# Probabilities times values in 64x64 tiles for the first four batches, and a new order of the work

## The chip, the cores and the metric

The kernel runs on one core of a Trainium2 chip. The metric is the device time of one execution in microseconds, lower is better. The core has five engines that run their own instruction streams in order: PE (TensorE, matmuls; its weight loads are shown apart as PEld), DVE (VectorE), ACT (ScalarE), POOL (GpSimd) and SP (SyncE, which issues the DMAs here).

## The reference

Eight batches of eight heads go through two attentions, with 32 learned rows `p` between them, and then through a gated projection. For each batch and head, with S = 576, D = 64 and 32 packed rows:

```python
p_packed = sm_attn(p, k, v)                 # 32 x 64: p attends to k, v
out = sm_attn(q, p_packed, p_packed)        # 576 x 64: q attends to the packed rows
x = out.transpose(0, 2, 1, 3).reshape(B, S, H * D)
gate = sigmoid(causal depthwise convolution of x with conv_w, 5 taps)
result = (gate * (x @ w_val)) @ w_out
```

`sm_attn` is softmax(q k^T / 8) v. The weights w_val, conv_w and w_out come as 64-bit words and are turned into float32 in the kernel.

## The kernel before

Each batch goes through a list of stages, each written as a Python generator, and each `yield` ends a step. A string ORDER names the stages by letters (with a batch number) and says how many steps of which stage come next: `a1.3` is three steps of `attn_pack` of batch 1. Every engine gets its instructions in the order in which the steps write them, since the class InOrder ties each instruction to the one before it on its engine. So ORDER alone sets what each engine does after what, the DMA issues of SP among it, and an instruction that waits holds up all that is behind it on its engine.

The stages that matter here, with the names that the profile gives their tiles:

- `load` (K, V, Q), `load_p` (P) and `load_weights` (L) issue the DMAs into km, vm, qm, p and the words tiles. At most five loads are under way at once (AT_ONCE).
- `value_weights` (W), `conv_weights` (C) and `out_weights` (O) turn the words into wv, cw and cwb, and woh and wol, in steps on ACT, DVE and POOL.
- `keys` (k) and `queries` (q) transpose p, km and qm on DVE into pT, kT and qT.
- `attn_pack` (a) is the first attention: `scores` on PE (s<-kT,pT), the row maxima on DVE (nb), the exponential on ACT (a), nine transposes on PE (at<-ident,a), two copies on ACT (a1t<-at), the product with the values on PE (pv<-vm,a1t), and ACT operations that scale it into ppd.
- `packed_turned` (p) transposes ppd on PE (ppTt) and copies it on ACT (ppT).
- `attn_out` (s), `weighted` (t) and `weighted_second` (u) are the second attention: `scores` on PE (s<-qT,ppT), then transposes, maxima and sums on DVE (t, mx, rs), two products on POOL and an exponential on ACT, and a transpose on DVE into a2 (a<-t).
- `mixed` (x) multiplies a2 by ppd on PE. Batches 0 and 1 (WHOLE) go through `convolved` instead: POOL multiplies ppd by the taps cwb (kx<-ppd,cwb), and 40 matmul calls for each half of the columns (x<-a,kx) give the convolution at once.
- `gate` (g), `packed_values` (w), `value` (v) and `project` (o) make the gate on DVE, multiply by w_val and by w_out on PE (wp, val, o), and put the result out through osb.
- `keep_busy` (D) issues 48 pairs of matmuls on the identity whose result is not used (spare<-ident).

A float32 matmul call is two passes on PE, each a weight load and a matmul instruction; a float32r call (o, val) and a transpose are one. The array works in tiles: a matmul with 64 rows and 32 columns of weights takes one of eight tiles, with 32 rows and 64 columns also one of eight, with 32 and 32 one of sixteen, with 64 and 64 one of four.

In the product with the values of the kernel before, nine chunks n of 32 keys, four head slots j and two groups g make 72 calls with weights of 64 x 32 and 64 moving columns each:

```python
pe.matmul(pv[heads[j], g, :D], a1t[rows, n, heads[j]],
          st["v", b][j // 2][rows, j % 2, n * D : n * D + D],
          start=(n == 0), stop=(n == NB9 - 1))
```

After it ACT writes ppd in four operations, two for each group, each a product with 1/sum (`sm`).

The functions that the change touches, as they stand before it:

Of the kernel before, what the change touches and what calls it, by code (L numbers as in the profile page):

```python
# [9 lines left out]
F32 = mybir.dt.float32  # L10
# [4 lines left out]
ALU = mybir.AluOpType  # L15
AX = mybir.AxisListType
# [38 lines left out]
ORDER = """
L0 W0 D0.2 K0 D0 P0 W0.3 L0 W0 D0 P0 k0 W0 K0 D0.2 W0.2 L0.2 W0 D0 W0.2 L0 W0.3 k0.2 D0 W0 D0 W0.3 L0 D0 W0.2 O0 
D0.5 W0.2 D0.5 O0 D0 a0.4 V0.2 a0 k1 O0.2 C0 O0 C0 D0.5 a0 D0 a0.3 D0 Q0 C0 W0.3 C0 W0.2 Q0 D0.3 a0.4 K1.2 D0 C0.2 
D0 q0.2 W0 C0 a0 k1 p0 O0.2 p0 s0 O0 C0 s0 C0.2 s0.2 D0.2 C0 k1 D0.2 x0 s0 a1 s0.2 a1 w0 V1 s0 a1 V1 a1 s0 D0.4 O0 
a1 t0 u0 a1 t0.2 D0 w0 a1 w0 a1 P2.2 D0.2 a1.2 u0 L0 O0 a1 u0 x0 O0.2 a1 t0.2 a1.2 O0 Q1 x0 u0 K2.2 p1 Q1 V2 x1 O0 
u0 k2.2 x0 O0 x0.2 D0 k2 a2 p1 q1.2 K3.2 x0 a2.3 v0 a2 k3 v0 k3 D0 O0.2 s1.2 | v0 O0 v0 a2 L0 O0 v0 s1 v0 a2 v0 a2.2   # L60
s1.2 D0 s1 V2 v0 k3 s1 v0.2 O0 v0 a3 O0 s1 a3.2 s1 a2 a3 O0.3 a3 t1.2 v0 V3 v0 u1 D0 O0 K4 a2.3 a3.2 Q2 q2 a2 t1 
w1 a3.2 w1 v0 P4 v0 V3 w1 u1.2 O0.2 p2.2 P4 k4.2 a3.3 L0 a3.2 v0 u1 O0 x1 u1 p3 x1 Q2 q2 t1 s2 O0.3 s2 O0 x1.2 t1 
x1.2 s2.4 K4 v1 k4 O0 s2 O0 s2 Q3 q3 Q3 v1 O0 a4 t2 a4 s2 a4 u2 p3 V6 O0 u2 a4 K5 q3 v1 V4.2 u2 a4 v1.3 o0 t2 s3 
a4 K5 o0 s3 u2.2 k5 a4.2 v1 Q4 s3.4 t2 x2 v1.2 s3 a4 v1.2 s3 v1.2 Q4 v1 x2.3 w2 x2 q4 k5 t2.2 t3 k5 t3 o0 x2 g8 x2 
g9.2 g10.2 g9 g8 g9 o0.2 v1 a4 v1 a4 o0.2 w2.2 s3 K6 u3 a4.3 u3 o0.2 g11 P6 q4 a5 p4.2 a5.2 g11 g8 o1 Q5 g9 g8 V5 
g11 s4 g8 s4 o1.3 g10 o1.2 g11 v2 V5 g10 g8 g11.2 o0 v2.2 a5 s4.2 a5 g9 P6 u3.2 o0 v2 s4.2 t3 v2.2 t3 g10 t3 u3 
g10 k6 a5 s4 v2.5 K6 Q5 k6.2 x3.4 o1 s4 q5 x3 o0 x3 g12.2 v2 o1 a5 o1 a5 v2 t4 a5 v2 o1 x3 g14 g12 g14 g13.2 v2 
g12 v2 q5 s4 u4 o1 w3.3 g15 t4 K7 a5 g12 a5 o2 g15 a5 V6 a6 g13 g15 g13 o2.2 g15 a5 o1 a5 g12 Q6 p5.2 Q6 g14 o2 v3 
g15 o2 g15 g14 a6 o1 g14 a6.3 v3 t4.2 o1 u4 s5 t4 v3 V7 g13 v3 o2 v3 u4 x4 s5 g13 s5 o1 s5 v3 g14 v3 u4 s5.3 v3.4 
s5 x4.2 a6 x4 o2 q6.2 x4.2 g16 o2 u4 x4 g19 w4 s5 v3.2 t5 o2 g16.2 v3 a6 v3.2 o3 K7 g19 u5 w4.2 u5 Q7 a6.3 g16   # L70
g18.2 g19 o3 g16 g17 a6 o3 g17 g19.2 o2.2 g16 u5.2 a6.2 v4.3 t5.3 g18 g17 g18 g17 g18 g17 a6 o3 x5.2 t5 o3 x5 k7 
o3 k7.2 p6.2 o3 u5 x5.2 g19 x5.2 g17 v4.2 o3 v4 o3 v4.2 g21 s6.4 o3.2 s6.2 g21.2 o3 v4 g21.2 g18 v4 q7 v4.4 g20.2 
V7 v4 Q7 o3 v4 o3 t6.2 a7.4 s6 o2 a7 o4.2 g20 s6 q7 g22 g20.2 g23.2 g22 o4 a7.4 o4 a7 o4 a7.2 o4 g22.2 g23.2 t6 
a7.2 s6 w5.3 p7.2 g22 u6 g20 o4.2 g22 u6 s7.2 g21 s7.3 v5.2 g23 v5.2 s7 g23 t6.2 u6.2 v5.3 o4.2 v5 x6.2 v5 u6 o4 
x6 o3 s7 x6 v5.7 x6.3 g26 t7 g26 o5.3 g26 w6.2 o5 g26 g27 w6 g24 v6 s7 g25 g24 o4 g25.2 s7 g27 g24 g27 g24 g27 g24 
o5.2 g25 o5.2 t7 g24 u7 v6 g26 g25 o5 g27 u7 v6.3 o5.3 g25 v6 g26 v6.3 g27 v6.3 x7 u7.2 o5.3 v6 t7.3 x7.3 v6.3 
x7.3 g28 g29.2 o6.2 g29 g28 o6 g30 w7 u7 w7.2 o6.2 g29 o6 g28 g29 g31 g28 v7 g29 o6.2 g30 g28 g30 g28 g30 v7.5 g30 
v7 g31 v7 g30 v7.3 g31 v7.2 g31.3 o7.3 v7.3 o7.2 o6 o7.14 o6.3 
"""


# [61 lines left out]
def packed_attention_gated_conv(  # L143
# [45 lines left out]
    NB9 = HS // NP
# [5 lines left out]
    const = ctx.enter_context(tc.tile_pool(name="const", bufs=1))  # L195
# [191 lines left out]
    def scores(name, of, xT):  # L387

        two = [big(f"{name}_{e}")[:, :, :HS] for e in range(G)]
        for h in range(2):  # L390
            for j in range(4):
                for e in range(G):
                    for c in range(2):
                        rows = heads[2 * e + c]
                        pe.matmul(
                            two[e][heads[j], c, :],
                            of(rows, j, h),
                            xT[j // 2][rows, j % 2, :, h, :],
                            start=(h == 0),
                            stop=(h == 1),  # L400
                        )
        return two
# [16 lines left out]
    def attn_pack(b):  # L419
        a1 = tile_of("a1", [P, NB9, G, 2, NP], F32, f"a1_{b}")  # L420
        sm = tile_of("sm1", [P, G], F32, f"sm1_{b}")
        s1s = scores(
            f"s1_{b}", lambda rows, j, h: st["pT", b][rows, j, h, :], st["kT", b]
        )
        yield
        for g in range(G):
            nb = tile_of("nb1", [P, 1], F32, f"nb1_{b}_{g}")
            dve.tensor_reduce(nb, s1s[g], axis=AX.XY, op=ALU.max, negate=True)
            yield
            act.activation(  # L430
                a1[:, :, g].rearrange("a m c i -> a c m i"),
                s1s[g].rearrange("a c (m i) -> a c m i", i=NP),
                AF.Exp,
                bias=nb,
                accum_out=sums[:, b, g, :1],
            )
            yield
        dve.tensor_reduce(sm, sums[:, b], axis=AX.X, op=ALU.add)
        dve.reciprocal(sm, sm)
        yield  # L440
        a1t = tile_of("a1t", [P, NB9, P], F32, f"a1t_{b}")
        at = big(f"at_{b}").rearrange("a u (n x) -> a (u n) x", x=P)
        at9 = one(f"at9_{b}")[:, :P]
        for n in range(NB9):
            pe.transpose(at[:, n] if n < NB9 - 1 else at9, a1[:, n].rearrange("a g c i -> a (g c i)"), ident)
        yield
        act.copy(a1t[:, : NB9 - 1], at)
        yield
        act.copy(a1t[:, NB9 - 1], at9)
        yield  # L450
        pv = big(f"pv_{b}")
        for n in range(NB9):
            for j in range(4):
                for g in range(G):
                    rows = slice(D * g, D * g + D)
                    pe.matmul(
                        pv[heads[j], g, :D],
                        a1t[rows, n, heads[j]],
                        st["v", b][j // 2][rows, j % 2, n * D : n * D + D],
                        start=(n == 0),  # L460
                        stop=(n == NB9 - 1),
                    )
# [12 lines left out]

    def keep_busy(b):
        spare = one("spare", "out")
        x = ident.bitcast(BF16)
        for _ in range(BUSY):
            for _ in range(2):  # L480
                pe.matmul(
                    spare.rearrange("a (n x) -> a n x", n=2),
                    x[:, :P],
                    x.unsqueeze(1).broadcast_to([P, 2, 2 * P]),
                    start=True,
                    stop=True,
                )
            yield
# [306 lines left out]
```

## Time and profile before

| what | us |
|---|---|
| median of 3 runs | 279.63 |
| lowest and highest | 279.4, 284.58 |
| the profiled execution | 281.81 |
| span of its instructions | 279.8 |

The profile is of one execution. The span runs from its first to its last instruction; 281.81 is the device time of that same execution. Times in the rows are microseconds from the start of the span, and "ns" where it says so. All matmuls stand on line 90 of the kernel, the helper that records each operation, so the rows are told apart by tile names. A name such as `pv` stands for the tile of any batch.

### The profile page before, as it was taken

The page shows a single profiled execution, that of the slowest core. Times are in us where ns is not written, and L with a number is a line of the kernel's source. Part 1 is how long each engine was busy: PE and PEld are TensorE (multiplying, and loading weights), DVE is VectorE, ACT ScalarE, POOL GpSimd, SP SyncE. Part 2 cuts the span into 40 slices and gives each one's busy share as a digit, 9 for nine tenths or more (in the row PEclk, how much of TensorE's full clock was granted, in tenths as well). Part 3 has the DMA queues.
Part 4 walks back from the last instruction along what each step waited for, and adds up shares of the span by engine and source line. Part 5 has one row for each costly group of instructions (what it writes and reads, how often), then busy time and mean ns, then how long its engine had stood idle before and what let it go on. Part 6 is the DMA issues. An engine that isn't in the chain of part 4 may idle for free.

```text
span 279.8 us, 8941 instructions
## 1 busy us (share of the span) xinstructions
PE 263.0 (94%) x3835; PEld 189.7 (68%) x3835; DVE 226.9 (81%) x319; ACT 165.7 (59%) x311; POOL 134.1 (48%) x130
## 2 busy tenths in 40 slices
PE   8879889989599999999999999999999999999994
PEld 3335455767257857797777688687778688679863
DVE  2598797798739899999999899989996699299810
ACT  4455276577436587287846795745657745954211
POOL 1546637378529983038505931555128413922420
PEclk9999999999979999999999999999999999999998
DMA  7999896865997304881576061026220111110014
GB/s 208 339 316 332 250 345 168 272 204 157 295 327 237 124 0 163 240 289 50 147 238 229 2 209 40 37 87 201 75 76 5 46 69 75 40 75 37 2 53 172
DMA packets 25733, 43.59 MB, mean 156 GB/s; under 512 B 6730, under 2 KB 6750, under 8 KB 25694
## 3 DMA queue, kind: packets, MB, share of 16 engines
q1 hardware_dynamic: 25694, 43.02, 47.1%
q8 instruction: 30, 0.49, 0.8%
q14 instruction: 9, 0.07, 0.1%
HBM read 33.57 MB, written 9.44 MB: 154 GB/s over the span
## 4 chain that ended last, share of the span: by engine, by line
PE 86%; DMA 5%; issue 3%; ACT 3%; DVE 1%; SPq 1%; ACTq 0%; DVEq 0%
PE o L90 37%; PE val L90 19%; PE s L90 9%; PE x L90 8%; PE pv L90 5%; PE at L90 3%; PE spare L90 3%; PE wp L90 3%; DMA wv_words<-in_moe_w_val_dram 2%; DMA wo_words<-in_moe_w_out_dram 2%; DMA p<-in_p_dram 2%; PE ppTt L90 1%; ACT a1t L90 1%; SPq L90 1%; ACT a L90 1%
## 5 line engine op out<-in xcount | busy, mean ns | idle before, releaser
L90 DVE SCALAR_TENSOR_TENSOR sig<-xp,cw,sig 128x576 f32<-128x576 f32 x96 | 77.6, 854 | 7.6 <-ACT sig L90 6.9
L90 POOL TENSOR_TENSOR gvl<-sig,gvh 128x576 fp32r<-128x576 f32 x32 | 46.7, 1462 | 31.9 <-ACT gvh L90 19.7
L90 PE MATMUL o<-woh,gvh 128*128 128x512 f32 x144 | 58.6, 407 | 0.8 <-ACT osb L90 0.7
L90 PE MATMUL o<-woh,gvl 128*128 128x512 f32 x144 | 56.8, 394 | 0.0
L90 PE MATMUL o<-wol,gvh 128*128 128x512 f32 x144 | 56.4, 392 | 0.0
L90 ACT ACTIVATE osb<-o 128x512 f32<-128x512 f32 x34 | 20.2, 595 | 32.7 <-PE o L90 27.9
L90 PE MATMUL val<-a2h,wph 128*128 128x288 f32 x128 | 39.1, 306 | 0.0
L90 PE MATMUL val<-a2h,wpl 128*128 128x288 f32 x128 | 37.7, 295 | 0.0
L90 PE MATMUL val<-a2l,wph 128*128 128x288 f32 x128 | 37.7, 295 | 0.0
L90 POOL TENSOR_TENSOR t<-t,rs 128x576 f32<-128x576 f32 x16 | 18.5, 1161 | 36.2 <-DVE sig L90 15.3
L90 PEld LDWEIGHTS o<-woh,gvh 128*128 128x128 f32 x144 | 27.0, 188 | 11.8 <-issue 3.1
L90 POOL TENSOR_TENSOR a2l<-a,a2h 128x576 fp32r<-128x576 f32 x16 | 22.7, 1426 | 19.8 <-DVE wo_words L90 8.6
L90 PEld LDWEIGHTS o<-woh,gvl 128*128 128x128 f32 x144 | 27.0, 188 | 6.6 <-POOL gvl L90 0.5
L90 PEld LDWEIGHTS o<-wol,gvh 128*128 128x128 f32 x144 | 27.1, 188 | 4.8
L90 ACT CAST gvh<-sig 128x576 fp32r<-128x576 f32 x32 | 21.5, 672 | 14.0 <-DVE sig L90 13.9
L90 DVE SCALAR_TENSOR_TENSOR sig<-sig,val 128x576 f32<-128x576 f32 x32 | 23.5, 740 | 7.1 <-PE val L90 5.7
L90 PEld LDWEIGHTS val<-a2h,wph 128*128 128x128 f32 x128 | 24.0, 188 | 5.1 <-issue 1.3
L90 POOL TENSOR_TENSOR t<-t,mx 128x576 f32<-128x576 f32 x16 | 18.6, 1162 | 18.6 <-DVE mx L90 13.7
L90 PE MATMUL spare<-ident 128*128 128x512 bf16 x96 | 24.4, 402 | 1.4 <-POOL ident masks.py:199 1.4
L90 PEld LDWEIGHTS val<-a2h,wpl 128*128 128x128 f32 x128 | 24.1, 188 | 0.5
L90 PEld LDWEIGHTS val<-a2l,wph 128*128 128x128 f32 x128 | 24.0, 188 | 0.0
L90 DVE STREAM_TRANSPOSE qT<-qm 128x1152 f32<-128x1152 f32 x16 | 21.5, 1355 | 0.6 <-DMA qm<-in_q_dram 0.6
(83 smaller groups left out, 436.5 us busy)
## 6 DMA issues: line engine op xcount, KB each, us to landing
km<-in_k_dram SPq DMA_DIRECT2D x32, 288.0 KB, 3.8
vm<-in_v_dram SPq DMA_DIRECT2D x32, 288.0 KB, 4.8
qm<-in_q_dram SPq DMA_DIRECT2D x32, 288.0 KB, 4.4
out_dram<-osb SPq DMA_DIRECT2D x36, 256.0 KB, 2.2
wv_words<-in_moe_w_val_dram SPq DMA_DIRECT2D x8, 256.0 KB, 3.8
wo_words<-in_moe_w_out_dram SPq DMA_DIRECT2D x8, 256.0 KB, 4.3
p<-in_p_dram SPq DMA_DIRECT2D x16, 64.0 KB, 4.1
cw_words<-in_moe_conv_w_dram SPq DMA_DIRECT2D x1, 20.0 KB
```

The lines of the kernel that those rows point to most:

```text
L90: made = getattr(self.engine, op)(*args, **kw)
```

## The change

Three things change.

1. For batches 0 to 3 a new function `paired` makes the product with the values. One call now takes two neighbouring heads: weights of 64 x 64 (the probabilities of both heads) against 128 moving columns (the values of both heads). That gives 36 calls in place of 72, and each row of pv gets its own head's 64 columns and its neighbour's. A table `parity`, made once on DVE, says which half is a row's own; `own` is 1/sum times that, zero for the wrong half. ACT multiplies the first half by `own`, DVE adds the second half times `own`, and ACT copies the result into the two places in ppd where before it wrote a product.
2. For batches 4 to 7 the same 72 calls stand in three steps of three chunks each.
3. ORDER is new throughout.

```diff
+ 'own': 1,
...
+PAIRED = (0,1,2,3,)
...
-L0 W0 D0.2 K0 D0 P0 W0.3 L0 W0 D0 P0 k0 W0 K0 D0.2 W0.2 L0.2 W0 D0 W0.2 L0 W0.3 k0.2 D0 W0 D0 W0.3 L0 D0 W0.2 O0 
+K0 L0.2 D0.2 W0.4 D0.2 P0.2 W0.2 L0 k0 W0.3 D0.2 W0.4 D0 k0 D0.2 K0 D0.2 W0.3 D0.2 Q0 D0 k0 L0.3 D0 V0.2 D0.2 W0.2 
...
+    parity = const.tile([P, 2], F32, name="parity")
+    of_pairs = ident.rearrange("a (m u n) -> a u m n", u=2, n=NP)
+    dve.tensor_reduce(parity, of_pairs, axis=AX.XY, op=ALU.add)
...
+        if b in PAIRED:
+            yield from paired(b, a1t, pv, sm)
+            return
...
-        yield
+            if n % 3 == 2:
+                yield
...
+    def paired(b, a1t, pv, sm):
+
+        for n in range(NB9):
+            for j in range(2):
+                two = slice(2 * NP * j, 2 * NP * j + 2 * NP)
+                for g in range(G):
+                    rows = slice(D * g, D * g + D)
+                    pe.matmul(
+                        pv[two, g, : 2 * D].rearrange("a (u d) -> a u d", u=2),
+                        a1t[rows, n, two],
+                        st["v", b][j][rows, :, n * D : n * D + D],
+                        start=(n == 0),
+                        stop=(n == NB9 - 1),
+                    )
+        yield
+        own = tile_of("own", [P, G, 2], F32, f"own_{b}")
+        dve.tensor_tensor(
+            own,
+            sm.unsqueeze(2).broadcast_to([P, G, 2]),
+            parity.unsqueeze(1).broadcast_to([P, G, 2]),
+            op=ALU.mult,
+        )
+        yield
+        ppd = st["ppd", b] = tile_of("ppd", [P, 3, P], F32, f"ppd_{b}")
+        for g in range(G):
+            plain = ppd[:, 2, g * D : g * D + D]
+            act.mul(plain, pv[:, g, :D], own[:, g, :1])
+            yield
+            dve.scalar_tensor_tensor(
+                plain,
+                pv[:, g, D : 2 * D],
+                own[:, g, 1:],
+                plain,
+                op0=ALU.mult,
+                op1=ALU.add,
+            )
+            yield
+        for g in range(G):
+            act.copy(
+                ppd[:, :2, g * D : g * D + D].rearrange("a h (c x) -> a h c x", c=2),
+                ppd[:, 2, g * D : g * D + D]
+                .rearrange("a (h x) -> a h x", h=2)
+                .unsqueeze(2)
+                .broadcast_to([P, 2, 2, NP]),
+            )
+        yield
```

Three places of the new order matter for the prediction. The first is PE after the first scores of the second attention (batch 0, tiles s_0_0 and s_0_1; cwps and spread belong to the conv weights, spare to keep_busy). Before:

```order
L90 MATMUL s_0_0_401<-qT_1_383,ppT_396 32x288 x2
L90 MATMUL s_0_1_402<-qT_1_383,ppT_396 32x288 x2
L90 MATMUL cwps<-ident,cw_top 128x20
L90 MATMUL spread<-cw_top,cwb 128x128 x5
L90 LDWEIGHTS ident
L90 MATMUL spare<-ident 128x512
```

And now, at the same place:

```order
L93 MATMUL s_0_0_379<-qT_1_347,ppT_368 32x288 x2
L93 MATMUL s_0_1_380<-qT_1_347,ppT_368 32x288 x2
L93 LDWEIGHTS ident
L93 MATMUL spare<-ident 128x512
L93 LDWEIGHTS ident
L93 MATMUL spare<-ident 128x512
L93 MATMUL s_1_0_428<-kT_0_362,pT_251 32x288 x2
L93 MATMUL s_1_1_429<-kT_0_362,pT_251 32x288 x2
```

The scores of batch 1 (s_1_0, s_1_1) stood behind cwps, spread and eight spare matmuls; now only two spare matmuls are between, and cwps, six spare, spread and wp follow them, ahead of the transposes `at` of batch 1.

The second place is DVE at the same time (kT_0 and kT_1 with km_0 and km_1 are the keys of batch 1, t_0 and mx_0 belong to the second attention of batch 0, nb_1 to the first of batch 1). Before:

```order
L90 STREAM_TRANSPOSE kT_0_388<-km_0_369 128x1152
L90 STREAM_TRANSPOSE t_0_398<-s_0_0_401 128x18x32
L90 COPY cw<-cwps 128x4x5
L90 TENSOR_REDUCE mx_0_399<-t_0_398 128x18
L90 STREAM_TRANSPOSE kT_1_453<-km_1_372 128x1152
L90 STREAM_TRANSPOSE t_0_398<-s_0_1_402 128x18x32
L90 TENSOR_REDUCE mx_0_399<-t_0_398 128x18
L90 TENSOR_REDUCE nb_1_0_500<-s_1_0_464 128x1
L90 TENSOR_REDUCE nb_1_1_519<-s_1_1_465 128x1
```

And now:

```order
L93 SCALAR_TENSOR_TENSOR ppd_344<-pv_287,own_342,ppd_344 128x64 x2
L93 TENSOR_TENSOR cw_top<-cw_top,cw_words 20x128
L93 STREAM_TRANSPOSE kT_0_362<-km_0_335 128x1152
L93 STREAM_TRANSPOSE kT_1_366<-km_1_338 128x1152
L93 STREAM_TRANSPOSE t_0_376<-s_0_0_379 128x18x32
L93 TENSOR_REDUCE mx_0_377<-t_0_376 128x18
L93 STREAM_TRANSPOSE t_0_376<-s_0_1_380 128x18x32
L93 TENSOR_REDUCE nb_1_0_462<-s_1_0_428 128x1
L93 TENSOR_REDUCE mx_0_377<-t_0_376 128x18
L93 TENSOR_REDUCE nb_1_1_468<-s_1_1_429 128x1
```

Both transposes of the keys of batch 1 now stand ahead of the transposes of the scores of batch 0, and the maxima of both batches alternate. The first row is the new operation of `paired`, twice.

The third place is the end of PE's program (o_3 is chunk 3 of the rows of batch 6, o_7 and o_8 are the last chunks of batch 7). Before:

```order
L90 MATMUL o_8_3798<-woh,gvh 128x512
L90 MATMUL o_8_3798<-wol,gvh 128x512
L90 MATMUL o_8_3798<-woh,gvl 128x512
L90 MATMUL o_3_3878<-woh,gvh 128x512
L90 MATMUL o_3_3878<-wol,gvh 128x512
L90 MATMUL o_3_3878<-woh,gvl 128x512
```

And now:

```order
L93 MATMUL o_7_3691<-woh,gvl 128x512
L93 MATMUL o_8_3692<-woh,gvh 128x512
L93 MATMUL o_8_3692<-wol,gvh 128x512
L93 MATMUL o_8_3692<-woh,gvl 128x512
L848 UNCONDITIONAL_BRANCH
```

The twelve matmuls of chunk 3 no longer end the program; they stand further ahead, before the products `val` of batch 7 are done.

## Rows read from the trace of the kernel before

**Rows 1.** The page's first part: busy time and share of each engine.

```profile
PE 263.0 (94%) x3835; PEld 189.7 (68%) x3835; DVE 226.9 (81%) x319; ACT 165.7 (59%) x311; POOL 134.1 (48%) x130
```

**Rows 2.** Chain of waits in time, 26 to 45: start, length, what.

```profile
26.54 1.64 PE s L90 x63
28.18 0.92 issue
...
29.34 1.21 PE spread L90 x10
30.54 1.83 PE spare L90 x8
32.38 1.53 PE s L90 x63
33.91 1.02 PE wp L90 x16
...
37.19 0.89 PE at L90 x8
...
39.22 1.51 PE pv L90 x93
40.74 1.04 issue
...
42.11 2.59 PE x L90 x80
```

**Rows 3.** The same chain, later pieces.

```profile
62.03 1.17 issue
...
72.03 3.45 issue
75.48 3.05 PE x L90 x63
...
81.26 0.80 DVE t L90
...
104.38 1.59 PE pv L90 x102
...
272.22 0.70 DVE osb L90
```

**Rows 4.** Stretches from the start into each issue wait: busy time (instructions), clock, DMA.

```profile
0.00:28.60 28.60, 23.46 (x350) 11.12 (x350) 18.47 (x31) 13.78 (x27) 12.73 (x19) 1.00 0.93 299
0.00:41.20 41.20, 34.91 (x605) 17.67 (x605) 29.04 (x49) 20.51 (x39) 20.08 (x25) 1.00 0.92 298
0.00:62.60 62.60, 55.16 (x1114) 31.85 (x1114) 46.75 (x73) 33.97 (x71) 33.09 (x36) 1.00 0.85 272
0.00:73.50 73.50, 63.79 (x1369) 37.79 (x1369) 55.76 (x88) 42.44 (x90) 42.79 (x44) 1.00 0.83 263
```

**Rows 5.** The page's DMA queues: packets, MB, share of 16 engines.

```profile
q8 instruction: 30, 0.49, 0.8%
```

**Rows 6.** Two stretches: PE, PEld, DVE, ACT, POOL busy, PE clock, DMA.

```profile
76.60:80.05 3.45, 3.45 (x74) 1.68 (x59) 0.00 (x0) 1.50 (x4) 0.00 (x0) 0.51 1.03 355
84.00:140.00 56.00, 56.00 (x890) 42.51 (x872) 54.38 (x77) 40.02 (x74) 33.25 (x32) 1.00 0.49 157
```

**Rows 7.** Groups of instructions: count, busy us, mean ns, idle before.

```profile
L90 PE MATMUL pv<-vm,a1t 64*32 64x64 f32 x1152 | 13.7, 225 | 2.4 <-issue 2.2 <-ACT a1t L90 0.2
L90 PEld LDWEIGHTS x<-a,kx 32*64 32x64 f32 x320 | 7.6, 135 | 8.2 <-issue 4.3 <-DVE t L90 0.7 <-ACT sig L90 0.7
L90 DVE COPY cw<-cwps 128x20 f32<-128x20 f32 x1 | 0.2, 179 | 0.4 <-PE cwps L90 0.4
L90 DVE SCALAR_TENSOR_TENSOR wo_top<-wo_top,wo_words 128x512 uint32<-128x512 uint32 x4 | 2.8, 689 | 0.2
L90 POOL TENSOR_TENSOR kx<-ppd,cwb 128x640 f32<-128x640 f32 x2 | 3.1, 1552 | 0.0
L90 ACT COPY cwb<-spread 128x640 f32<-128x640 f32 x1 | 0.7, 692 | 4.1 <-PE spread L90 4.1
```

More of the change, by code (lines that the diff above doesn't have):

```diff
@@ L55 @@
 ORDER = """
-L0 W0 D0.2 K0 D0 P0 W0.3 L0 W0 D0 P0 k0 W0 K0 D0.2 W0.2 L0.2 W0 D0 W0.2 L0 W0.3 k0.2 D0 W0 D0 W0.3 L0 D0 W0.2 O0
[L57 to L75, printed above, removed]
@@ L76 @@
-o5.2 g25 o5.2 t7 g24 u7 v6 g26 g25 o5 g27 u7 v6.3 o5.3 g25 v6 g26 v6.3 g27 v6.3 x7 u7.2 o5.3 v6 t7.3 x7.3 v6.3
-x7.3 g28 g29.2 o6.2 g29 g28 o6 g30 w7 u7 w7.2 o6.2 g29 o6 g28 g29 g31 g28 v7 g29 o6.2 g30 g28 g30 g28 g30 v7.5 g30
-v7 g31 v7 g30 v7.3 g31 v7.2 g31.3 o7.3 v7.3 o7.2 o6 o7.14 o6.3
+K0 L0.2 D0.2 W0.4 D0.2 P0.2 W0.2 L0 k0 W0.3 D0.2 W0.4 D0 k0 D0.2 K0 D0.2 W0.3 D0.2 Q0 D0 k0 L0.3 D0 V0.2 D0.2 W0.2
+D0 W0 D0.4 C0 D0.2 a0.5 C0 W0.2 q0 D0 W0 C0 k1 D0.2 O0 a0.2 Q0 D0.4 O0 a0.3 W0 C0 W0 C0 W0 O0 W0 D0.2 K1.2 O0 a0.2
@@ new lines @@
+O0 q0 a0.2 O0 a0.2 p0 C0.2 O0 k1 D0 k1 p0 P2.2 s0 L0 W0 s0.2 D0 O0.2 s0.3 a1.3 s0 C0 a1 D0 W0 D0 C0 s0 D0 t0.2 C0
+a1 s0 w0.2 a1.3 D0 C0 u0.2 x0 V1 D0.2 V1 a1 w0 K2 O0 u0 O0 a1 t0 O0 a1 O0.2 a1.4 O0 t0 k2.2 K2 Q1 x0 Q1 k2 a1 x0
+p1.2 u0 q1.2 V2 u0 t0 O0 x0.4 D0 a2.2 D0 a2 O0.2 a2 x1 D0 a2 K3 k3.2 K3 Q2 v0.2 | v0 k3 s1.2 v0 s1.2 v0.3 s1.2 v0.3
+V2 s1.2 a2 t1 a2.2 a3 a2 L0 O0.3 a2 s1 t1 a3.2 L0 a3 a2.2 O0 a2 P4 a3 O0 u1 Q2 a3 a2.2 O0 u1 O0.2 v0 D0 a2 D0 t1
+P4 v0 O0 v0.2 a3.3 D0 u1 w1 v0.2 V3.2 q2 p2 w1 a3.3 w1 k4 q2 a3.3 t1 p2 K4 k4 u1 a3 x1.3 p3 t1 O0 K4 O0 Q3 u1 s2
@@ new lines @@
+k4 V4 s2 O0 D0 s2.5 x1.3 O0 s2 Q3 q3 O0 V4 O0.2 v1.2 x2 O0.2 K5 p3 q3 v1.2 s2 a4.3 v1 t2 a4.2 k5 Q4 v1 o0 u2 K5 t2
+o0 a4 t2 a4 k5 a4 v1 u2 t2 u2 s3 Q4 v1.2 s3 v1.2 s3.3 P6 s3 V6 o0.2 q4 x2 o0 u2 o0 v1 x2.2 q4 s3 t2 v1.2 u2 v1 s3
+w2.2 x2.2 g8 g9 o0 a4 o0 a4.4 t3 v1 o1 x2 g10 P6 k5 a4.2 w2 a5 s3 g8 Q5 o1 K6 g8 g9 V5 g8 g9.2 a4 o0 p4 g10 p4 g8
+g10 g9.2 a5.4 o0 g10.3 Q5 t3 u3.2 s4.3 o0 v2 g11 u3 t3 a5 o1 a5.2 t3 o1 s4 g11.3 g8 v2 o1.2 v2.2 g11 s4.3 v2 s4
+u3.2 o1.2 x3.3 v2 x3 s4 k6 v2.3 q5.2 x3.2 v2 o0 w3 x3 K6 t3 v2.3 g15 t4 u4 g14 w3 k6 a5 t4 o1.2 k6 V5 a5 u4 g12 a5
@@ new lines @@
+g11 w3 o1 v2.3 g12 u4 a5.4 t4.2 a5 g14 o2.2 g15.2 o2 a6 g14 g12 t4 g13 a6 p5.2 o2 a6.2 g14 a6 g13.2 g12 o2 g13
+g12.2 g13 g15 v3.2 o1.2 s5 g14 s5 o1 s5 u4 v3.2 K7 v3 g14 s5 g13 s5 v3 a6 g15 s5.2 o2.2 u4 x4 v3 x4.4 s5 x4 g17 x4
+o2 v3 Q6 v3 q6 g17 v3 g15 v3 g17 s5 V6 v3.3 o2 v3.2 a6 t5 u5 g16 o3 g16 a6 w4 o3 a6 g16 a6.2 g19 g17 g19 a6 u5
+w4.2 a6 g19 g16.2 t5 o3.3 g16 u5 v4.2 g18 V7.2 a6 o2 g17.2 a6 g18.2 g19 g18 o3 o2 a6 u5 g18 t5 g18 t5 g19.2 u5
+v4.3 o1 o3 x5.4 v4.2 o3 K7 Q6 k7.3 v4.2 q6 v4 x5.2 p6 x5 t5 p6 g23.3 o3.2 g23 v4 g20.2 o3.2 s6.3 v4.4 s6.2 g22
@@ new lines @@
+s6.2 t6 v4 o3.2 g23.2 o2 a7 t6 a7 Q7.2 g20 a7 g21 a7.2 g22 q7.2 a7 w5 o4 a7 o4.3 s6 g22 s6 g21 a7 g20 a7.2 o4 a7
+w5 u6 w5 a7 o4.2 u6 t6 g21 a7.4 g20 p7.2 t6 g20 g21.2 v5.3 t6 s7.3 v5 g21 o4 s7.3 v5.2 g22 o3 g22 v5 g22 o4 v5.2
+x6 o4 u6 x6 v5 u6.2 s7 v5.2 x6 v5.2 x6 s7 x6 o4 v5.2 o5 x6 g24.2 o4 g24.2 x6 g24 g25 o5 w6.3 g27.2 s7 g27 g26 o5
+g26 g24 g25 g26 g25 g26 g27 o5.2 v6 o5 v6 o5.2 g26 g27 g25.2 v6 o5 x7 g26 v6.2 o5 t7.2 g27 g25 o5 u7 v6.2 u7 t7.2
+v6.8 o5.2 t7 u7 x7 o5 x7 o5 x7 v6 x7.2 g29.3 x7 g28.3 o6.2 w7.3 u7.2 g28 o6.4 g28 g29 v7 g29 g28 g30.2 o6 g29 o6
@@ L79 @@
+v7.3 g30 g31 v7 g31 g30 o6 v7 o6.3 g30 v7.3 g31.2 g30 g31.2 v7.7 o7.19
 """
```

## The prediction

> **What bounds the kernel now.** I read the page's busy shares first: PE is busy 94% of the span, DVE 81% [rows 1]. Busy does not mean useful, since the spare matmuls count too, so the second view is the chain of waits in order of time. It runs on PE almost throughout. From 84 to 140 us PE is busy all 56.00 us and DVE 54.38, or 97% [rows 6], and the chain shows only PE work until the tail. So the time is what PE has to do from about 26 us on, plus the places where PE stands.
>
> Those places are what the reader should look for in the chain: four pieces named "issue", in which PE waits for no engine, of 0.92, 1.04, 1.17 and 3.45 us [rows 2, 3], together 6.58. The third view says what they are. I asked for stretches that end inside each of them and read PE's instruction counts. PE has then done 350, 605, 1114 and 1369 matmuls and as many weight loads [rows 4], that is 700, 1210, 2228 and 2738 instructions. The distances are 510, 1018 and 510: two, four and two times 256, less a few semaphore instructions that the counts omit. The instruction queue moves 30 packets in 0.49 MB [rows 5], so 16 KB each, and PE's 2 x 3835 instructions [rows 1] make 30 blocks of 256. So PE stands at the ends of instruction blocks whose successor is late.
>
> They are late where PE eats a block fast or where the DMA engines are full. The product pv is 1152 / 8 = 144 passes a batch [rows 7], 288 instructions in 1.59 us when nothing disturbs it [rows 3], more than a block. The 1.04 and the 1.17 lie inside pv, the 3.45 in the 17th instruction pair behind one. The 0.92 follows scores instead, while the DMA engines are 93% busy [rows 4].
>
> The long wait costs more than itself: the granted clock is 0.51 from 76.60 to 80.05 [rows 6], the level of 1.2 GHz, right after PE had stood for 3.45 us. Half of 3.45 us of work is 1.7 us lost.
>
> **The change part by part.** All sums stand against the profiled execution's 281.81 us (its span of 279.8 and 2.0 around it). The median of the three runs is 279.63, so 2.2 us lower; I take it that the 3.45 and the clock are larger in the profiled execution than usual.
>
> The 64x64 tiles halve pv's instructions to 144, in 72 passes over four tiles, so 18 passes a tile as before, but with 128 columns in place of 64. No row shows this shape. For float32 passes, x makes 10 a tile of 288 columns in 2.59 us (0.90 ns a column), wp 2 of 512 in 1.02 (1.0 ns), at 8 of 128 on the whole array in 0.89 (0.87 ns), s 4 of 288 in 1.53 (1.33 ns) [rows 2]. For 18 x 128 columns these give 2.0 (at), 2.1 (x), 2.3 (wp) and 3.1 (s). The lower end is half of 1.59 = 0.8, if the instruction count set pv's time. I take 2.15, near x and at, whose weights have as many columns or more: +0.55 a batch, bounds -0.8 and +1.5. Batches 2 and 3 stand on PE's path: 2 x 0.55 = +1.1. Batches 0 and 1 are inside the next sum.
>
> The scaling keeps four ACT operations and adds two DVE operations a batch and the small `own`. A DVE operation is at least 0.18 (cw) and at most 0.69 us (wo_top) [rows 7]; I take 0.25, so 8 of them and 4 `own` of 0.18 are some 2.7 us of DVE, beside PE except in batch 0, where the transposes ppTt wait for them. There I add 0.6 to the path. In the other three batches x or val of another batch stands on PE between pv and ppTt (x alone is 2.59 [rows 2]) and hides them.
>
> The new order of the head. Up to pv of batch 0 both orders do the same work, with loads exchanged; I take no difference, bounds of one weight conversion, 0.7, either way [rows 7]. Then scores of batch 0's second attention begin at 26.54 + 0.6 = 27.1, hold 1.64 and end at 28.7. Scores of batch 1 began at 32.38 behind the 0.92, spread and eight spare; now two spare (0.23 each by 1.83 / 8) precede them, so 29.2. From their start to `at` it took 37.19 - 32.38 = 4.81 before [rows 2], with DVE's maxima and the exponential in it: 34.0. But cwps, six spare (1.4), spread (1.21) and wp (1.02) now stand between on PE: 29.2 + 1.5 + 3.6 = 34.3, and I take 34.4. The step from at to pv was 39.22 - 37.19 = 2.03: pv at 36.4, plus 2.15 = 38.6. Then x needs kx, whose taps are copied behind the first a1t copy: 36.4 + 0.69 + 1.55 [rows 7] = 38.7. So x starts at 38.7 where it was 42.11: -3.4. This contains the 0.92 and the 1.04. But the block end at 700 instructions now lies in scores of batch 1, at 30 to 31 us, in the time of full DMA engines, where it cost 0.92 before. I put 0.8 there: -2.6.
>
> The later block waits. The 1.17 and the 3.45 with its clock go: -6.3. With 144 instructions in 2.15 us, pv takes 15 ns an instruction in place of 5.5. The block end behind pv of batch 3 has the least work ahead of it now, pv and then x, some 3 us for 200 instructions, where before it was 1.1 to 1.5. I leave 1.3 us for what stays there: +1.3.
>
> Spare matmuls. Behind pv of batch 1 there were 8, now 14. Six of 0.23 are +1.4, partly in waits that PE has anyway (the 0.80 for DVE's t [rows 3] has two of them in front now): +1.2.
>
> The tail. Chunk 3 no longer ends the program, so PE no longer waits 0.70 for osb [rows 3] before it: -0.7. Its matmuls are the same work elsewhere.
>
> pv in three steps: the 72 calls of batches 4 to 7 still stand together on PE, so 0. If anything were between them, it would be work that is needed anyway.
>
> Sum: 1.1 - 2.6 - 6.3 + 1.3 + 1.2 - 0.7 = -6.0, or 275.8. I forecast 276.0, 1.3% under the median.
>
> One rule of the Trainium skill speaks against the main term. Its page Runtime: NRT & Kernel Launch, section Instruction fetch mechanics, has the engine fetch blocks of 16 KiB ahead by itself, and says the cost of crossing one is mostly hidden. The trace agrees on the 256 instructions [rows 4, 5] and not on the hiding: 6.58 us stand at four of 30 ends. By the page these waits would have another cause and fewer instructions would not remove them, which is the first rival.
>
> **The rivals.**
>
> First, the change doesn't do what it says: block waits come back at other places. For it speaks that the 0.92 came without a dense pv, and that the 3.45 is far longer than the two inside pv, so how full the DMA engines are decides too. Against it, 26 of 30 ends cost nothing. Then the 1.17, the 3.45 and the 1.7 return, less the 1.3 that I left: +5.0, or 281.
>
> Second, DVE binds. It is 97% busy from 84 to 140 [rows 6] and gets 2.7 us more. If PE comes 5 us earlier and DVE can't, PE waits there. Against it, DVE stood as well while PE stood at 72 us, so it comes earlier too. Then the gain of the head is lost: 276.0 + 2.6 = 278.6.
>
> Third, slower: the weights of the four tiles are not hidden. With a field of 2 x 2 tiles in place of 2 x 4, a tile's next load may have to wait for its stream. A load of 64 columns takes 135 ns [rows 7], a stream 115 by x's rate: 18 x 250 = 4.5 us, +2.35 a batch on four batches = +9.4, or 285.4. It is slower than the median from a pv of about 3.1 us on. Against it: with the same 135, pv of today would take 18 x (58 + 135) = 3.5 and takes 1.59. The skill's page TensorE: Matmul & The Clock Gate, section Part 3: Packing small matmuls, has loads overlap running matmuls only where the row group differs, which is this case; today's pv, also in two row groups, doesn't bear it out.
>
> Fourth, the instruction count sets pv: 0.8 us, 4 x 1.35 = 5.4 less, 270.6. Against it, x and wp follow their columns.
>
> **How the numbers follow.** My forecast gets 0.47 (own range 273 to 278.5), block waits elsewhere 0.20, DVE 0.18, the loads 0.07, the count 0.08. Two per cent of the median, about what a measurement of this kernel can tell from no change, is 5.6 us: faster means under 274.0, slower over 285.2. Faster: the 0.08 of the count and a third of the forecast's 0.47, 0.24. Slower: over half of the 0.07 and 0.02 for what I don't see, 0.06. Same: 0.70. The range of 272 to 281.5 leaves out the third and fourth rival and little else.
>
> **What would show it.** Right: pv of batches 0 to 3 at 2.0 to 2.3 us each; x of batch 0 starting at 38 to 40 us; no "issue" piece over 1.5 us and a clock of 1.00 through 80 us; no wait for osb before the last products. Wrong: pv at 0.8 or over 3; issue pieces that add up to over 4 us; PE waits for DVE between 84 and 200, where there were none.

## The result and the profile after

The changed kernel takes 276.58 us (median of 4 runs, 276.27 to 277.98); the kernel before took 281.36 us in the same comparison (4 runs, 279.40 to 284.58). The ratio is 0.988, 95% interval 0.984 to 0.993: faster by 1.2%, less than the 2% that separate "faster" from "same". The ratio is taken over the faster executions of each kernel, so it says 1.2% where the medians are 1.7% apart, and the profiled execution of the kernel before (281.81 us) is one of its slower ones. The profiled execution of the changed kernel took 276.28 us, its span is 274.3; the pieces below are differences between these two executions, 5.5 us in all, and not of medians.

The page after, busy shares and instruction queue, against [rows 1, 5]:

```profile
PE 263.6 (96%) x3547; PEld 192.0 (70%) x3547; DVE 229.1 (84%) x332; ACT 167.4 (61%) x311; POOL 133.7 (49%) x130
...
q8 instruction: 28, 0.46, 0.7%
```

PE is busy as long as before with 288 matmuls fewer, and two instruction blocks fewer are fetched. The groups of instructions that are new (count, busy us, mean ns, idle before):

```profile
L93 PE MATMUL pv<-vm,a1t 64*64 64x128 f32 x288 | 9.0, 272 | 0.1
L93 DVE SCALAR_TENSOR_TENSOR ppd<-pv,own,ppd 128x64 f32<-128x64 f32 x8 | 2.2, 273 | 1.1 <-ACT ppd L93 1.1
L93 DVE TENSOR_TENSOR own<-sm,parity 128x4 f32<-128x4 f32 x4 | 0.8, 206 | 0.0
```

What PE waited for in the whole run, first and fifth line of seven (us in total, times, longest):

```profile
PE ppTt L93 <- ACT ppd L93: 2.0, 2, 1.3
...
PE o L93 <- ACT osb L93: 0.7, 1, 0.7
...
```

None of the seven lines says "issue": all four waits for instruction blocks are gone. New is the first line, ppTt behind the scaling. The chain of waits (start, length, what) in the head, against [rows 2], and around the new wait:

```profile
22.75 5.54 DMA km<-in_k_dram
...
28.38 1.38 DVE kT L93
...
30.48 1.57 PE s L93 x59
...
35.94 1.13 PE at L93 x9
...
38.42 2.31 PE pv L93 x70
40.73 2.59 PE x L93 x80
...
68.77 0.43 DVE pT L93
69.20 1.26 DVE qT L93
70.46 0.18 DVE ppd L93
...
72.94 0.55 PE ppTt L93 x3
...
100.62 1.59 PE pv L93 x102
```

The x of batch 0 starts at 40.73 where it was 42.11 [rows 2], so 1.4 of the 5.5 us come before it and 4.1 after it. The 1.4 is uncertain by about as much: in three more kernels below whose programs are the same up to there (the trials with qT and with small spares, and all batches paired) this x starts at 41.00, 40.37 and 42.39. The granted clock is 1.00 in every stretch to the last products:

```profile
28.50:84.00 55.50, 53.77 (x1128) 37.37 (x1102) 50.86 (x81) 35.92 (x80) 38.88 (x35) 1.00 0.85 270
84.00:140.00 56.00, 55.83 (x860) 41.80 (x860) 54.49 (x78) 39.59 (x75) 30.47 (x29) 1.00 0.47 150
```

Note DVE in the first of these stretches (columns: length, then busy us of PE, PEld, DVE, ACT, POOL): 50.86 of 55.5 us, 92%. It returns below.

### The profile page after: what moved, and what is told of

It is laid out like the page before. It is cut to its first block, busy times and chain, and to the rows that moved or that the text cites. A ratio compares the mean times of both kernels' runs of the same rounds, so it can differ in the third digit from the quotient of the medians.

```text
span 274.3 us, 8380 instructions
## 1 busy us (share of the span) xinstructions
PE 263.6 (96%) x3547; PEld 192.0 (70%) x3547; DVE 229.1 (84%) x332; ACT 167.4 (61%) x311; POOL 133.7 (49%) x130
## 4 chain that ended last, share of the span: by engine, by line
PE 83%; DMA 10%; ACT 2%; DVE 2%; issue 1%; SPq 0%; DVEq 0%; ACTq 0%
PE o L93 37%; PE val L93 20%; PE s L93 8%; PE x L93 6%; PE pv L93 4%; DMA qm<-in_q_dram 4%; DMA km<-in_k_dram 3%; PE wp L93 3%; PE at L93 3%; PE spare L93 2%; DMA wo_words<-in_moe_w_out_dram 2%; DMA wv_words<-in_moe_w_val_dram 2%; PE ppTt L93 1%; DVE kT L93 1%; PE spread L93 0%
## 5 line engine op out<-in xcount | busy, mean ns | idle before, releaser
L93 POOL TENSOR_TENSOR gvl<-sig,gvh 128x576 fp32r<-128x576 f32 x32 | 46.1, 1445 | 36.5 <-ACT gvh L93 28.4
L93 PE MATMUL val<-a2h,wph 128*128 128x288 f32 x128 | 39.7, 310 | 0.0
L93 ACT ACTIVATE osb<-o 128x512 f32<-128x512 f32 x34 | 20.2, 595 | 29.2 <-PE o L93 24.1
L93 PE MATMUL spare<-ident 128*128 128x512 bf16 x96 | 25.7, 415 | 1.4 <-POOL ident masks.py:199 1.4
L93 ACT ACTIVATE sig<-sig 128x576 f32<-128x576 f32 x24 | 16.3, 684 | 11.8 <-DVE sig L93 11.7
```

The lines of the kernel that those rows point to most:

```text
L93: made = getattr(self.engine, op)(*args, **kw)
```

## The experiments

**One part at a time.** The theory was that fewer instructions remove the block waits, and that the order comes second. First the pairs without the new order:

```diff
 (kernel before, its ORDER)
+        if b in PAIRED:
+            yield from paired(b, a1t, pv, sm)
+            return
...
             act.mul(plain, pv[:, g, :D], own[:, g, :1])
-            yield
             dve.scalar_tensor_tensor(
...
```

> The kernel before with its own order, and batches 0 to 3 in 64x64 tiles (the two additions of the scaling share their steps, so that the order fits). Theory, that fewer instructions move the block ends out of pv: the ends at 955 to 2738 instructions then lie in x, scores and wp; the issue waits of 1.04, 1.17 and 3.45 us go with the 1.7 us of half clock, one of up to 1 us stays in the head, each pv takes 2.1 to 2.3 us (+0.7 on the path for three batches, +0.6 for the additions of batch 0): about 4.5 us less than before, a ratio near 0.984. Rival, that the new order brings the gain: ratio 0.995 to 1.01, and issue waits that still add up to over 4 us.

Measured: 283.14 us, ratio 1.017 (1.008 to 1.025). Slower than before; neither theory nor rival gave that. The early block waits did go. Two other things took their place, in the groups of DVE and in the chain of this kernel:

```profile
L93 DVE SCALAR_TENSOR_TENSOR ppd<-pv,own,ppd 128x64 f32<-128x64 f32 x8 | 2.2, 270 | 6.6 <-ACT ppd L93 6.6
```

```profile
103.22 1.59 PE pv L93 x102
...
136.74 1.30 issue
```

DVE stood 6.6 us in front of the eight additions, against 1.1 in the changed kernel: the old order has it come to each addition while ACT has not yet scaled the first half, and the transposes that PE needs next are queued behind. And a block wait of 1.30 us has appeared in pv of batch 5, where the kernel before had none.

Then the order without the pairs:

```diff
 (changed kernel, its ORDER)
-PAIRED = (0,1,2,3,)
+PAIRED = ()
...
-            if n % 3 == 2:
+            if n % 3 == 2 and b > 3:
                 yield
+        if b < 4:
+            yield
+            yield
...
```

> The changed kernel with its new order, and no batch paired: pv of all batches in 144 passes, the steps left empty stand where the additions stood. Theory: block ends fall at 23 and 278 of 288 instructions of pv of batch 1, at 196 in that of batch 2, at 70 in that of batch 3 and 19 pairs into x behind it, nearly where they were before, so the issue waits come back (1 us, 1 us and 3 us or more, and a clock below 1.00 behind the longest): 2 to 6 us over the changed kernel, 278 to 281 us, ratio 0.99 to 1.005. Rival, that the order alone brings the gain: 275 to 276.5 us, since each pv is 0.7 us shorter, and no issue wait over 0.9.

Measured: 285.08 us, ratio 1.023 (1.016 to 1.030). The waits came back, and one is longer than any before. Its chain:

```profile
27.94 0.95 issue
...
39.46 3.48 issue
...
43.37 5.00 PE x L93 x80
...
65.44 1.18 issue
...
75.57 1.83 issue
```

The first stands in the second attention's scores of batch 0, as the 0.92 did before. Stretches that end inside the second and the third (PE's matmuls in the first bracket, the clock third from the end):

```profile
0.00:41.00 41.00, 35.62 (x605) 17.52 (x605) 29.11 (x51) 21.22 (x40) 20.22 (x25) 1.00 0.95 301
0.00:66.00 66.00, 58.11 (x1114) 32.43 (x1114) 46.46 (x75) 33.62 (x69) 34.28 (x37) 0.95 0.84 266
```

The counts are those of the kernel before, 605 and 1114 [rows 4], again in pv of batch 1 and of batch 2; the fourth lies in x behind pv of batch 3. Behind the 3.48 the next x took 5.00 us in place of 2.59: the clock again, 0.50 from 43.40 to 48.30. So the order alone loses 2.3%, the pairs alone 1.7%, and both together gain 1.2%. The two are not terms of a sum.

**Whose waits are they?** To move the block ends and nothing else, the first spare matmuls of the kernel before, where PE waits for loads anyway, were cut into pieces of the same total columns: 64 matmuls more (half a block), or 128 (a whole one).

```diff
+            parts = 4 if step < 10 else 2 if step < 12 else 1
             for _ in range(2):
-                pe.matmul(spare ... 512 columns)
+                for part in range(parts):
+                    pe.matmul(spare ... 512 // parts columns)
```

(the whole block: 21 and 22 in place of 10 and 12.)

> The kernel before with its first 12 pairs of spare matmuls cut into four or two pieces of the same total columns: 64 more matmuls and as many weight loads, so 128 instructions, half a block, ahead of everything that matters; nothing else is changed. Theory, block ends: the waits stay at 700 + k x 256 instructions of PE and so come 128 instructions earlier in the work: 138 of 288 into pv of batch 1 (up to 1 us), 194 into pv of batch 3 (about 1.2 us), none at the 17th pair of x behind pv of batch 3, and no wait of over 2 us; with the clock this is 3 to 4 us less than before, ratio near 0.988. Rival, that the waits belong to the work at those places (a buffer, a transfer, a tile): 1.04, 1.17 and 3.45 us stay where they were in the work, ratio 1.00.

> As the half block, but with 128 more matmuls and weight loads, 256 instructions, a whole block. Theory: the block ends fall on the same work as in the kernel before, two instructions earlier, and the waits come back there: about 1 us in pv of batch 1, 1.2 in pv of batch 2, 3 or more in x behind pv of batch 3, and the clock falls behind it; ratio 0.997 to 1.003. If the half block is faster only because the start of the program was changed, this one is faster too, by as much or more, ratio 0.99 or less.

Measured: half 282.08 us, ratio 1.003 (0.996 to 1.011); whole 280.82 us, ratio 1.002 (0.997 to 1.007). Stretches that end inside waits, half a block:

```profile
0.00:45.50 45.50, 38.15 (x732) 24.30 (x733) 32.02 (x53) 22.63 (x45) 21.33 (x26) 1.00 0.90 277
0.00:74.50 74.50, 64.71 (x1369) 42.54 (x1369) 53.75 (x85) 40.25 (x84) 39.00 (x42) 0.98 0.82 253
```

and a whole block:

```profile
0.00:40.80 40.80, 35.66 (x733) 24.95 (x733) 29.02 (x49) 20.47 (x39) 20.07 (x25) 1.00 0.94 298
0.00:62.20 62.20, 55.90 (x1242) 39.10 (x1242) 46.97 (x73) 33.99 (x71) 33.09 (x36) 1.00 0.87 274
0.00:72.70 72.70, 64.51 (x1497) 44.97 (x1497) 55.84 (x87) 42.42 (x90) 42.23 (x44) 1.00 0.84 264
```

With a whole block the waits stand at 733, 1242 and 1497 matmuls, each 128 more than 605, 1114 and 1369, so at the same work as before (0.81, 1.41 and 2.17 us in the chain, and behind the 2.17 the clock is 0.57 from 73.96 to 77.90). With half a block they stand at 733 and 1369 again, on the same grid, and so at other work: 2.52 us in x of batch 0 and 0.70 in pv of batch 3. A third, 1.03 us in the chain, stands at 350 matmuls as before, now ahead of the second attention's scores of batch 0 and no longer behind them. The place follows the count of instructions and not the work; that part of the theory is shown. The price was wrong: half a block saved nothing. In the profiled execution (282.53 us) the end at 733 cost 2.52 us in x, where I had expected none, and the clock is 0.73 from 46.96 to 53.30 behind it. The ratio is the rival's, though the places are not.

**Does the load of the DMA engines decide?** The kernel before with fewer loads under way:

```diff
-AT_ONCE = 5
+AT_ONCE = 3
```

> The kernel before with 3 loads under way at once in place of 5. Theory, that a block comes late because it queues behind the loads: the waits at 1210, 2228 and 2738 instructions (1.04, 1.17, 3.45 us) shrink, the three together to under 3 us; the loads themselves come later, so the start of x of batch 0 moves behind 42 us and the total may be longer. Rival, that PE's own rate alone makes them late: the three waits stay within 20% of 5.66 us together.

One execution: 287.13 us. Two of the waits are left, at the same 1114 and 1369 matmuls; PE's waits of this kernel:

```profile
PE x L90 <- issue: 1.5, 1, 1.5
PE pv L90 <- issue: 1.4, 1, 1.4
```

Together 2.9 us where it was 5.66 for three, and the 3.45 has become 1.5. The loads came later and cost more than that. It fits a block that queues behind loads, though the work around the waits moved as well, so this is support and not proof.

**How many pairs does it take?** If only the place of the block ends matters, two paired batches can do for four, and pairs where no block end costs anything should bring nothing.

```diff
-PAIRED = (0,1,2,3,)
+PAIRED = (1,3,)
...
 (or, alone, (0,1,2,3,4,5,6,7,))
```

With two pairs, the empty steps of the run without pairs stand in for the additions of batches 0 and 2.

> The changed kernel with only batches 1 and 3 paired. Theory, that only the place of the block ends counts and not how many batches are paired: the ends then lie at 955 instructions in the paired pv of batch 1, at 1973, 85 of 288 instructions into pv of batch 2 with scores ahead of it, at 2228 in spares, at 2482 in x behind the paired pv of batch 3; one at 700 comes back at the end of the scores of batch 0 (0.9 us). No issue wait over 1.0, clock 1.00 through 84 us, batches 0 and 2 save 0.6 us of PE and 0.7 of VectorE each: 275 to 276.6, ratio 0.981 to 0.988. Rival, that each unpaired batch brings its wait back: 279 to 282, ratio 0.995 or more.

Measured: 277.20 us, ratio 0.986 (0.980 to 0.991), so as good as the changed kernel within the intervals. The wait foretold at 700 instructions came, longer than foretold (1.45 for 0.9), and the clock that was to stay at 1.00 is 0.63 from 29.15 to 33.00; in pv of batch 2, with its 144 passes and a block end in it, nothing waits. The chain:

```profile
27.70 1.45 issue
...
60.76 1.51 PE pv L93 x97
```

> The changed kernel with batches 4 to 7 in 64x64 tiles too, same order. Theory: behind 84 us no block end costs PE anything in the changed kernel, so the halved instructions save nothing there; four pv take 2.15 in place of 1.59 us, +2.2, and 12 more operations run on VectorE, which is 97% busy there: 2 to 3.5 us over the changed kernel, 278.6 to 280, ratio 0.995 to 1.00. Rival, that fewer instructions help everywhere: at or under 276.6, ratio 0.988 or less.

Measured: 291.05 us, ratio 1.038 (1.031 to 1.045), so 14 us over the changed kernel where I expected 2 to 3.5. Its group of additions, the stretch from 84 to 140, and its chain there:

```profile
L93 DVE SCALAR_TENSOR_TENSOR ppd<-pv,own,ppd 128x64 f32<-128x64 f32 x16 | 4.3, 270 | 7.4 <-ACT ppd L93 7.4
```

```profile
84.00:140.00 56.00, 51.11 (x557) 37.99 (x556) 47.12 (x70) 32.94 (x60) 27.41 (x26) 0.94 0.43 138
```

```profile
106.07 1.32 DVE kT L93
...
109.44 3.02 DVE sig L93 x4
...
112.48 3.75 DVE sig L93 x5
...
116.94 0.83 ACT a L93 x2
...
117.81 2.55 PE s L93 x60
```

DVE loses 7.4 us in front of the additions, and what is queued behind them, nine steps of the gate among it, comes late to ACT, whose exponential PE's scores wait for (4.7 us); the clock is 0.50 from 117.80 to 124.00 behind that wait. DVE is less busy there than in the changed kernel (47.12 against 54.49 us) and yet the chain runs over it: by this it was the waits, and not the durations of the new operations.

The same lesson backwards, on the pairs in the old order, with both additions later in DVE's queue:

```diff
             act.mul(plain, pv[:, g, :D], own[:, g, :1])
-            dve.scalar_tensor_tensor(plain, ...)
             yield
+        yield
+        for g in range(G):
+            dve.scalar_tensor_tensor(plain, ...)
```

> The pairs in the old order once more, but both additions stand in the fifth step in place of the second and third, so that VectorE comes to them behind other work (the two qT of batch 0, an a of batch 0, and wo_words). In the first run with pairs in the old order VectorE waited 6.6 us for ScalarE's ppd in its six longest waits there, in the changed kernel 1.1. Theory, that the added wait on VectorE, with everything queued behind it, ate the gain: these waits fall under 3 us, and 2 to 5 us come back, ratio 0.985 to 1.005. Rival, that the loss lies elsewhere in the old order (loads, spare matmuls): ratio still 1.01 or more.

Measured: 282.69 us, ratio 1.011 (1.007 to 1.016). DVE's waits fell as the theory has it, and the ratio is the rival's, 1.01 or more, with an interval that reaches a little below it. The group and the chain:

```profile
L93 DVE SCALAR_TENSOR_TENSOR ppd<-pv,own,ppd 128x64 f32<-128x64 f32 x8 | 1.8, 270 | 2.4 <-ACT ppd L93 2.4
```

```profile
101.52 1.59 PE pv L93 x102
...
134.96 1.46 issue
```

DVE's waits fell from 6.6 to 2.4, and pv of batch 4 starts at 101.52, 1.7 us before the first run with pairs in the old order and 2.9 before the kernel before (104.38 [rows 3]). So the theory holds to batch 4. The end does not keep it: block waits of 1.46 in pv of batch 5 and 1.09 in pv of batch 7 (2.5 in all in PE's waits) eat most of the lead. My first rival, waits that come back elsewhere, is what happens to the pairs in the old order.

**What is a paired pv worth?** The pairs with 64 moving columns in place of 128, so that half of the products is left out.

```diff
-                        pv[two, g, : 2 * D].rearrange("a (u d) -> a u d", u=2),
+                        pv[two, g, :D],
                         a1t[rows, n, two],
-                        st["v", b][j][rows, :, n * D : n * D + D],
+                        st["v", b][j][rows, 0, n * D : n * D + D],
```

> The changed kernel, but the 64x64 tiles multiply only the first of the two heads' 64 columns, so half of the products is left out and the scaling adds the same half twice; instructions, weight loads and order stay. If the columns set the time of a paired pv (18 passes a tile x 128 columns), it falls from 2.13 to 2.31 us to some 1.1 to 1.3, the group's mean from 272 ns to under 250, and PE's path gets 2 to 3 us shorter where nothing else holds it. If the weight loads set it (18 x 135 ns a tile, one behind the other), it stays over 2.0.

One execution: 276.15 us. The group of its paired pv, and the start of pv of batch 4 in its chain:

```profile
L93 PE MATMUL pv<-vm,a1t 64*64 64x64 f32 x288 | 5.1, 221 | 0.1
```

```profile
100.36 1.59 PE pv L93 x102
```

9.0 us have become 5.1, so 0.97 us less a pv for 18 x 64 columns less, 0.84 ns a column: the columns set it, and the weight loads do not. But 3.9 us less of PE moved pv of batch 4 by 0.3 us and the end by 0.1. PE's waits for ppd rose in their place, from 2.0 to 3.0 us.

**Can it be beaten?** Three trials on the changed kernel.

```diff
-... w1 k4 q2 a3.3 t1 p2 K4 ...
+... w1 k4 a3.3 q2 t1 p2 K4 ...
```

> The changed kernel with one step of the order moved: the second transpose qT of batch 2 (1.26 to 1.33 us on VectorE) stands behind the two additions of ppd of batch 3, no longer ahead of them. Theory: the transposes ppTt of batch 3 no longer wait 1.27 us for ppd, PE's path gets 0.7 to 1.2 us shorter, ratio 0.983 to 0.986. Rival: ScalarE's a2h, ppT and copies ahead of ppd hold it anyway, or the scores of batch 2 now wait for qT: within 0.3 us of the changed kernel, ratio 0.987 to 0.989.

Measured: 276.38 us, ratio 0.985 (0.980 to 0.990), not to be told from the changed kernel by these intervals, though 0.985 is in the theory's range. The wait for ppd of batch 3 fell from 1.3 to 0.4, but in this execution pv of batch 3 began only when its values had landed, 0.8 later; ppTt and the end did not move. Its chain:

```profile
62.11 5.54 DMA vm<-in_v_dram
...
67.69 2.21 PE pv L93 x68
...
100.60 1.59 PE pv L93 x102
```

On top of that, the 14 spare matmuls behind pv of batch 1 with 16 columns in place of 512:

```diff
+            wide = 2 * P if step < 41 else 8
...
-                    x.unsqueeze(1).broadcast_to([P, 2, 2 * P]),
+                    x[:, :wide].unsqueeze(1).broadcast_to([P, 2, wide]),
```

> The kernel with qT behind the additions, and the spare matmuls behind pv of batch 1 (14 of 512 columns, some 0.24 us each) cut to 16 columns; their number and so the block ends stay where they are. Theory, that they stand on PE's path as my prediction had it (+1.2 for six more of them): of the 2.05 us of spares that the chain shows behind x of batch 0, 1.0 to 1.6 come back, ratio 0.980 to 0.983. Rival: VectorE, 92% busy from 40 to 84 us, and the values of batch 3, which land at 67.65 us just as their pv starts, set the pace there, so PE only waits in place of running spares: within 0.4 us of the kernel without this cut, ratio 0.984 to 0.987; or, if the added idle time lowers the granted clock, slower.

Measured: 277.58 us, ratio 0.991 (0.987 to 0.995): no gain. Its chain has pv of batch 3 1.6 us earlier than that, and the lead is gone at batch 4:

```profile
66.06 2.12 PE pv L93 x72
...
100.27 1.59 PE pv L93 x102
```

Last, the load of the first output weight behind the keys of batch 1, its first seven conversion steps later:

```diff
-... D0 k0 L0.3 D0 V0.2 ... k1 D0.2 O0 a0.2 Q0 ... K1.2 O0 a0.2 O0 q0 ...
+... D0 k0 L0.2 D0 V0.2 ... k1 D0.2 a0.2 Q0 ... K1.2 L0 a0.2 q0 ...
```

> The changed kernel with the load of the first output weight (0.5 MB, needed only from 84 us on) behind the keys of batch 1 and its seven first conversion steps spread over 30 to 65 us. Theory: what holds the start of the program is the queue of loads; everything behind this load lands 1.4 to 1.8 us earlier (the keys of batch 1 at 26.7 in place of 28.3), x of batch 0 starts at 39.2 to 39.8 in place of 40.7, and the end comes 0.8 to 1.5 us earlier, ratio 0.982 to 0.986. Rival: the start is held by the engines' own chain, or the conversions now stand in the way of ScalarE and VectorE at 30 to 65 us: 276 to 278, ratio 0.988 or more.

Measured: 285.66 us, ratio 1.019 (1.013 to 1.025). The second half of the rival came true, and its price was far too low (278 at most). The theory failed too: x of batch 0 starts at 42.44 where 39.2 to 39.8 was foretold. The chain before the second half of x of batch 0:

```profile
45.04 1.29 POOL wol L93
...
46.36 0.67 ACT wo_top L93
...
47.68 2.67 PE x L93 x76
```

With one buffer for the weight's upper part, ACT's next conversion stands behind POOL's last one, and the tanh that frees PE's accumulators stands behind ACT's conversion.

## Why the prediction was right, and where it was not

The forecast was 276.0 and the range 272 to 281.5; 276.58 was measured, and the profiled execution lost 5.5 us where the sum said 6.0. The main mechanism was right; that the sum came so close is in part luck, since misses of one to two us each way cancel in it. By its steps:

- **The block waits** (-6.3, with 1.3 left over for what stays). Right in mechanism, shown by the whole and the half block. All four went, with the half clock, and nothing of the 1.3 was needed. But "the 1.17 and the 3.45 with its clock go" read as if fewer instructions did it. It takes the places of the block ends that pairs and order give together: without the pairs the new order has 1.18, 1.83 and even 3.48 us, with only two pairs it is as fast, and with the pairs the old order gets new ones in batches 5 and 7.
- **pv paired** (+1.1). The size was right, 2.13 to 2.31 us against 2.15, and by its columns, so the third and the fourth rival fall. As a term on the path it was not: with 0.97 us less for each pv the end moved by 0.1.
- **The scaling**. The durations were right (273 ns against 250, 206 against 180). That x or val of another batch stands on PE between pv and ppTt and hides them failed in batch 3: ppTt waited 1.3 us, because pT and qT stood ahead of the first addition on DVE, and then a2h, ppT and a2h ahead of ppd's copies on ACT; with the second qT behind the additions 0.4 is left. I had priced the operations and not the queue: in the old order the same additions made DVE wait 6.6 us.
- **The head** (-2.6). It gave -1.4. The step that failed is the way from the start of the scores of batch 1 to `at`, 4.81 before and 5.2 in the forecast. They started at 29.41, as forecast (29.2), but only four matmuls of them: the other 60 waited until 30.48 for DVE's t, the transpose that takes the scores of batch 0 out of their accumulator. The new order puts t behind the second kT, whose keys landed at 28.29. So `at` came at 35.94 and not 34.4. The sum also leaves out the 0.55 that it puts on a paired pv for batch 0; that pv began 0.7 earlier than before (22.21 for 22.91), which hides it. The 0.8 for a block wait there was not needed: the end at 700 lay in spare matmuls.
- **The spares** (+1.2). Not on the path: cutting them gave nothing.
- **The tail** (-0.7). Right: DVE's osb is gone from the chain. The sign that I gave for it, no wait for osb before the last products, was too wide: ACT's wait of 0.7 remains, as before.
- **Three steps** (0). Right: pv of the later batches takes 1.59.

So the head gave 1.2 less than the sum. From x of batch 0 to pv of batch 4 the chain took 59.89 us for 62.27 before, and it holds more work: the new order puts 36 matmuls o there in place of 24, and o behind pv of batch 4 is shorter by 2.76 us in the chain. On equal work this stretch gained 5.1, where the sum had 2.7. It would come out as the 6.3 of waits and clock less the new 1.3, with nothing for pv, spares and leftover waits, but no run shows these terms one by one. Behind pv of batch 4 the kernel gained 1.7 with that work gone, so on equal work it lost 1.0, where the sum gains 0.7 from the tail: PE twice waits for ACT's xp, 1.3 us in the chain and none before, and val takes 0.7 longer. No term of the sum was for either. All this rests on one profiled execution of each kernel.

Between x of batch 0 and pv of batch 4 something else than the amount of PE's work sets the pace of the new order. In six kernels, with two, four or eight batches paired, with half the columns, with qT moved or with small spares, this stretch takes 59.6 to 60.2 us: what the head loses or gains arrives whole at pv of batch 4, and 2.8 us less of spares does not show there. DVE is 92% busy from 28.5 to 84, and the loads of values land just in time. Which of the two, and where, no run here separates. So my second rival, DVE, may bound the gain, though not where I put it (84 to 200 us). One of its arguments was misread: while PE stood at 72 us DVE was busy for 2.78 of the 3.45 us, and stood behind that, from 76.60 to 80.05 [rows 6].

The first rival's 281 was close by: the changed kernel avoids the waits by where its ends happen to lie, and why those ends cost nothing is open.

The Trainium skill's page Runtime: NRT & Kernel Launch, section Instruction fetch mechanics, calls the cost of a block end "mostly hidden". The traces agree for 26 of 30 ends in the kernel before and for all in the changed kernel. The others followed the count of instructions through every kernel in which they were counted, with 0.2 to 3.5 us each.

## What to carry to other kernels

When a wait ends with no engine to blame, count the instructions before it: if the counts lie on a grid of blocks, shift the grid by a few cheap instructions and see whether the wait follows, before any other cause is argued. An added operation on an in-order engine costs its place in the queue and not its duration: eight additions of 0.27 us cost 1.1 or 6.6 us of standing by the order around them. Two changes that were tuned together need to be tested apart and together, because here each alone is slower and only both are faster.

## What was not expected of the hardware

- A block end may cost 1.0 or 3.5 us at nearly the same work. The end at 605 matmuls took 1.04 us in the kernel before and 3.48 with the new order and no pairs, both in pv of batch 1. The end behind the second attention's first scores took 0.92 and, with a whole block more ahead of it, 0.18.
- How early the next block is fetched differs. In the pairs in the old order with late additions the packet ran when 2062 matmuls were done, in the middle of pv of batch 5, and PE stood 1.46 us. In the changed kernel the packet before pv of batch 5 ran at 127.7 us, when 1990 were done and pv had not begun (130.30), and nothing stood. What makes a fetch early or late is open; no run was made for it.
- After PE had stood 3.48 us the granted clock fell again: the x behind it took 5.00 us in place of 2.59, at a granted clock of 0.50, the level of 1.2 GHz, from 43.4 to 48.3 us.
